# Seven-for-eight products of w_out for all batches of chunks 2 to 5, in an mLSTM cell with a cosine-gated feed-forward block

## The chip, the cores and the metric

The kernel runs on one core of one Trainium2 chip. The time is the device time of one execution in microseconds. Of the kernel before there are three runs, with a median of 536.95 us (536.02 to 537.94), and one profiled execution.

## The reference

Two blocks follow each other. The first is an mLSTM cell over 768 steps for 4 batches and 8 heads of 40 values: a state that decays by a forget gate and takes up an outer product at each step, is read with q, normalized and multiplied by an output gate. The second is a feed-forward block on its 3072 rows of 320 values. This change touches only the last product, that with w_out:

```python
x = np.ascontiguousarray(attn_out.transpose(0, 2, 1, 3)).reshape(B * S, H * D)   # (3072, 320)
h = x @ w_in                        # w_in (320, 2048)
g = h * np.cos(h)
return (g @ w_out).astype(np.float32)   # w_out (2048, 320)
```

All of it is in float32.

## The kernel before

**Tiling.** The 768 steps are cut into NC = 6 chunks of 128 steps; a cell is one chunk of one batch (all 8 heads), so there are 24 cells. The feed-forward block works on a chunk of all four batches at once, 4 x 128 = 512 rows. Its 2048 hidden values are 16 blocks of 128, taken two at a time: f2 = 0 to 7, each a pair.

**One slot.** For a pair, class Up multiplies x^T with the two blocks of w_in (L624 and L627) into two PSUM banks, the only two of the pool ps_u. ACT rounds (L632), DVE takes the fraction (L635), ACT takes the sine (L640), and DVE multiplies (L644, method gate) into the gated block g, 128 hidden values x 512 rows. gate reads the two banks last, so the next Up can have them only after that. I call the time of one Up and the work beside it a slot, T = 8c + f2 for chunk c.

**Order.** The order is written out by hand: both_parts(c, b) records an even slot (f2 = 2b) and an odd one (2b + 1), and each engine works through its own instructions in that order. Beside chunk c run the cells of chunk c + 1, a cell for each pair of slots. In an even slot TensorE does Up, the scores of the cell (L450), a step of w_out, then the values (L487, L493, into the two banks of pool ps_a which the scores also use); DVE does L635, weighs the scores (L456), subtracts for the next cell's decay (L372), multiplies the gates, and later normalizes (L507 to L519). In an odd slot TensorE does Up, the state's products (L589) and a step of w_out; DVE does L635, the state (L605), the gates, and transposes for the next cell (L411). Chunk 5 has no cells beside it, so its slots hold only Up and a step.

**x^T over DRAM.** The last 8 values of each head go from the normalized cell to DRAM (L523) and back (L526) into the third part of xT, which L627 reads.

**The product with w_out.** A step is `down(c, f2)`: it adds the pair's contribution for all four batches. In chunk 0 it is eight products of 320 columns (L757). From chunk 1 on, down_parted does batches 2 and 3 in that way (whole, four products of 320 columns), and batches 0 and 1 by Strassen's scheme in Winograd's form: the 2 x 2 blocks are two batches by the two blocks of the pair, and the two blocks by two halves of w_out's columns. Seven products P1 to P7 of 160 columns take the place of eight. They need four sums of blocks of g (`sums`, POOL, L683, in tiles "sg" of which there are two) and four differences of blocks of w_out for each pair (POOL, L662, made once in chunk 1). The products add up over all eight pairs in PSUM: P1, P2 and P6 in one bank of pool ps_o, P5, P3 and P4 in another, P7 beside batch 2's sum in a third; four banks in all. After the eighth pair ACT copies P1 (L726), seven additions on DVE (L731) make the two batches' rows, and ACT copies the whole ones (L708); SP stores them (L745).

down(c, f2) stands one slot after the pair's gates: pair f2's step is done in slot 8c + f2 + 1. So after the last Up two steps are done: pair 6, in the last slot, and pair 7 alone.

Of the kernel before, what the change touches and what calls it, by code (L numbers as in the profile page):

```python
# [11 lines left out]
FP = mybir.dt.float32  # L12
# [4 lines left out]
OP = mybir.AluOpType  # L17
# [6 lines left out]
TWO_PI = 2.0 * math.pi  # L24
# [5 lines left out]
def kernel(  # L30
# [20 lines left out]
    nc = tc.nc  # L51

    B, H, S, D = q.shape
    C = 128
    NC = S // C
# [3 lines left out]
    DM = H * D  # L59
    DFF = moe_w_in.shape[1]  # L60
    NF = DFF // 128
# [11 lines left out]
    const = ctx.enter_context(tc.tile_pool(name="const", bufs=1))  # L73
    wp = ctx.enter_context(tc.tile_pool(name="wp", bufs=1))
    p2 = ctx.enter_context(tc.tile_pool(name="p2", bufs=2))
    p3 = ctx.enter_context(tc.tile_pool(name="p3", bufs=3))
    p4 = ctx.enter_context(tc.tile_pool(name="p4", bufs=4))
    pb = ctx.enter_context(tc.tile_pool(name="pb", bufs=5))
# [3 lines left out]
    ps_u = ctx.enter_context(tc.tile_pool(name="ps_u", bufs=2, space=bass.MemoryType.PSUM))  # L82
    ps_o = ctx.enter_context(tc.tile_pool(name="ps_o", bufs=4, space=bass.MemoryType.PSUM))
# [48 lines left out]
    def parts(dst, bits):  # L132
        n = dst.shape[1]
        hi, lo = bits[:, 0:n, 1], bits[:, 0:n, 0].bitcast(U32)
        t = p2.tile([128, WQ], I32, name="wt", tag="wt")[:, 0:n]
        m = p2.tile([128, WQ], I32, name="wm", tag="wm")[:, 0:n]

        nc.scalar.activation(out=t.bitcast(FP), in_=hi.bitcast(FP), func=AF.Abs)

        nc.scalar.activation(out=m, in_=lo, func=AF.Copy, scale=2.0 ** -29)  # L140
        return dst, hi, t, m
# [139 lines left out]
        nc.scalar.copy(out=tab[:, 1, 2], in_=pg[:, 2 * R])  # L281
        nc.scalar.copy(out=tab[:, 1:R, 3], in_=pd)

    gp = ctx.enter_context(tc.tile_pool(name="gp", bufs=6))


    N = NC * B
# [320 lines left out]
    gs, po = {}, {}  # L608

    class Up:  # L610
# [23 lines left out]
        def rest(self, e):  # L634
            nc.vector.scalar_tensor_tensor(out=self.n[e].bitcast(FP), in0=self.pu[e], scalar=0.25, in1=self.n[e],  # L635
                                           op0=OP.add, op1=OP.subtract)
# [3 lines left out]
            nc.scalar.activation(out=r, in_=r, func=AF.Sin, scale=TWO_PI_DOWN)  # L640

        def gate(self, e):
            g = gp.tile([128, B * C], FP, name="g", tag="g")
            nc.vector.scalar_tensor_tensor(out=g, in0=self.pu[e], scalar=TWO_PI, in1=self.n[e].bitcast(FP),  # L644
                                           op0=OP.mult, op1=OP.mult)
            gs[self.c, 2 * self.f2 + e] = g

    DH = DM // 2
    Ts, sg = {}, {}

    def parted(c):
        return c > 0

    def differences(p, T):

        B11, B12, B21, B22 = (w_out_sb[:, 2 * p + e, ts(h, DH)] for e in range(2) for h in range(2))  # L660
        for i, (x, y) in enumerate(((B12, B11), (B22, T[:, 0]), (B22, B12), (T[:, 1], B21))):
            nc.gpsimd.tensor_tensor(out=T[:, i], in0=x, in1=y, op=OP.subtract)  # L662
        Ts[p] = T

    def two_differences(p):

        if p < 6:
            T = pc.tile([128, 2, 4, DH], FP, name="T", tag="bits")
            for e in range(2):
                differences(p + e, T[:, e])  # L670
        else:
            for e in range(2):
                differences(p + e, pb.tile([128, 4, DH], FP, name="T", tag="bits"))

    def sums(c, f2):

        if not parted(c):
            return
        S = p2.tile([128, 4, C], FP, name="sg", tag="wt")
        A11, A21, A12, A22 = (gs[c, 2 * f2 + e][:, ts(b, C)] for e in range(2) for b in range(2))  # L680
        for i, (x, y, op) in enumerate(((A21, A22, OP.add), (S[:, 0], A11, OP.subtract),
                                        (A11, A21, OP.subtract), (A12, S[:, 1], OP.subtract))):
            nc.gpsimd.tensor_tensor(out=S[:, i], in0=x, in1=y, op=op)  # L683
        sg[c, f2] = S

    def down_parted(c, f2):
        end = f2 == NF // 2 - 1
        if f2 == 0:

            po[c] = [ps_o.tile([128, 3 * DH + 32], FP, name="po", tag="o") for _ in range(4)]  # L690
        P1, P2, P6, P5, P3, P4 = (po[c][i // 3][:, ts(i % 3, DH)] for i in range(6))
        P7 = po[c][2][:, DM:DM + DH]
        g0, g1 = (gs[c, 2 * f2 + e] for e in range(2))
        w0, w1 = (w_out_sb[:, 2 * f2 + e] for e in range(2))
        S, T = sg[c, f2], Ts[f2]
        lo, hi = slice(0, DH), slice(DH, DM)

        def product(out, g, w, first=False):

            nc.tensor.matmul(out, g, w, start=(f2 == 0 and first), stop=end, skip_group_check=True)  # L700

        def whole(b):
            for e, (g, w) in enumerate(((g0, w0), (g1, w1))):
                product(po[c][b][:, 0:DM], g[:, ts(b, C)], w, e == 0)

        def whole_out(b):
            o = p2.tile([128, DM], FP, name="o_sb", tag="o_sb")
            nc.scalar.copy(out=o, in_=po[c][b][:, 0:DM])  # L708
            result(c, b, o)

        very_end = end and c == NC - 1
        if not very_end:
            for b in range(2, B):
                whole(b)
        product(P1, g0[:, 0:C], w0[:, lo], True)
        product(P2, g1[:, 0:C], w1[:, lo])
        product(P6, S[:, 1], T[:, 1])
        product(P7, S[:, 2], T[:, 2])
        product(P5, S[:, 0], T[:, 0], True)
        product(P3, S[:, 3], w1[:, hi])  # L720
        product(P4, g1[:, C:2 * C], T[:, 3])
        if not end:
            return None
        o2 = p2.tile([128, 2, DM], FP, name="o2", tag="wm")
        U = p1.tile([128, 2, DH], FP, name="hs", tag="hs")
        nc.scalar.copy(out=U[:, 0], in_=P1)  # L726
        for dst, x, y, op in ((o2[:, 0, lo], U[:, 0], P2, OP.add), (U[:, 0], U[:, 0], P6, OP.add),
                              (U[:, 1], U[:, 0], P7, OP.add), (U[:, 0], U[:, 0], P5, OP.add),
                              (o2[:, 0, hi], U[:, 0], P3, OP.add), (o2[:, 1, lo], U[:, 1], P4, OP.subtract),
                              (o2[:, 1, hi], U[:, 1], P5, OP.add)):  # L730
            nc.vector.tensor_tensor(out=dst, in0=x, in1=y, op=op)  # L731
        if very_end:
            for b in (3, 2):
                whole(b)

        def rest():
            for b in range(2):
                result(c, b, o2[:, b])
            for b in (3, 2):
                whole_out(b)  # L740

        return rest

    def result(c, b, o):
        nc.sync.dma_start(out=out[b * S + c * C:b * S + (c + 1) * C], in_=o)  # L745

    def down(c, f2):
        if parted(c):
            return down_parted(c, f2)
        if f2 == 0:  # L750
            po[c] = [ps_o.tile([128, DM], FP, name="po", tag="o") for _ in range(B)]

        order = [(f, b) for f in (2 * f2, 2 * f2 + 1) for b in range(B)]
        if f2 == NF // 2 - 1:
            order.sort(key=lambda fb: fb[1])
        for f, b in order:
            nc.tensor.matmul(po[c][b], gs[c, f][:, ts(b, C)], w_out_sb[:, f], start=(f == 0), stop=(f == NF - 1))  # L757
            if f == NF - 1:
                o = p2.tile([128, DM], FP, name="o_sb", tag="o_sb")
                nc.scalar.copy(out=o, in_=po[c][b])  # L760
                result(c, b, o)

    spot = const.tile([1, 1], FP, name="spot")
    nc.gpsimd.memset(spot, 0.0)
# [146 lines left out]
    def both_parts(c, b):  # L911
# [6 lines left out]
        begin = c == b == 0  # L918
        more = cell and n + 1 < N
        f2 = 2 * b  # L920
        up = Up(c, f2, cell_after_first if begin else None)
        if cell:
            scores(n)
# [14 lines left out]
        for e in range(2):  # L938
            up.sin(e)
            up.gate(e)  # L940
        sums(c, f2)
        if n == TURNED:
            turn_gates(n)
        if c == 0 and b == 1:
# [7 lines left out]
            out_join(*out_parts())  # L952
        if pieces:
            h = parts(*pieces.pop(0))
        rest = None
        if b == 0 and c > 0 and parted(c - 1):
            rest = down(c - 1, NF // 2 - 1)
        if begin or more and c > 0:
            decay(n + 1)
        elif more:  # L960
            decay_by_bias(n + 1)
        if f2 > 0:
            down(c, f2 - 1)
        elif rest:
            rest()
        elif c > 0:
            down(c - 1, NF // 2 - 1)
        if cell:
            if n + 2 < N:
                load(n + 2)  # L970
# [21 lines left out]
        sin_next()  # L992
        if pieces:
            h = parts(*pieces.pop(0))
        up = Up(c, f2 + 1)
        if cell:
            seam(n)
# [10 lines left out]
        for e in range(2):  # L1008
            up.sin(e)
            up.gate(e)  # L1010
        sums(c, f2 + 1)
        if more:
            weigh_k(n + 1)
        if c == 1 and b < B - 1:
            two_differences(2 * b + 2)
        if pieces:
            join(*parts(*pieces.pop(0)))
        down(c, f2)
        if pieces:
            join(*parts(*pieces.pop(0)))  # L1020
        if c == 0:
# [8 lines left out]
        if c == 0:  # L1030
            out_join(*h)
            if b == B - 1:
                two_differences(0)
                sigmoid(2)
                sin_next()
# [4 lines left out]
    with tc.manual_schedule():  # L1040
        first_cells()
        for c in range(NC):
            for b in range(B):
                both_parts(c, b)
        down(NC - 1, NF // 2 - 1)()


# [28 lines left out]
```

## Time and profile before

| | us |
|---|---|
| median of three runs | 536.95 |
| profiled execution | 536.09 |
| its span | 534.4 |
| Up (L624, L627), busy | 175.1 + 54.2 |
| w_out, chunk 0 (L757), busy | 36.6 |
| w_out, chunks 1 to 5 (L700), busy: 320 columns; 160 columns | 96.7; 39.4 + 28.3 + 17.4 + 17.4 |
| sums of g on POOL (L683), busy | 36.6 + 18.3 + 18.3 |
| gates on DVE (L644), busy; mean of one | 61.7; 0.684 |

The span is the profiled part of the execution; 1.7 us (536.09 - 534.4) lie outside it. Busy times of TensorE overlap each other, [...]so their sum is no measure of the span; starts of successive rows are the better measure. Each product of the program stands as two rows on TensorE: eight products of L757 are x16.

In pairs of slots, the starts of Up in the chain of waits are 20.62 us apart in chunks 1 to 3 and 20.19 in chunk 4; in chunk 5 each slot takes 8.74 us. DVE is busy 15.1 to 16.8 us of a pair, POOL 9.7 in chunk 1 and 5.7 in chunks 2 and 3.

### The profile page before, as it was taken

Reading aid. Unit: us, or ns where it says so; the run is one execution under the profiler, and the core shown is the slowest. Engines: PE = TensorE matmul, PEld = TensorE weight load, DVE = VectorE, ACT = ScalarE, POOL = GpSimd, SP = SyncE. Lnnn points to the kernel's source line nnn. Section 1 sums busy time; section 2 is a strip of 40 time slices with the busy share of each in tenths; the row PEclk is TensorE's granted clock in tenths of the full one; section 3 lists DMA queues with packets and bytes.
Section 4 is the critical chain, followed back from the end, with each engine's and each line's share of the span. In section 5 each row is a group of like instructions: output and inputs, shape, how many; then the busy total and the mean of one; then the engine's idle time right before and its main releaser. Section 6 shows DMA issues by size and latency. Waiting matters only on the chain.

```text
span 534.4 us, 10042 instructions
## 1 busy us (share of the span) xinstructions
PE 525.4 (98%) x3669; PEld 331.5 (62%) x3669; DVE 370.5 (69%) x734; ACT 262.2 (49%) x416; POOL 168.5 (32%) x305
## 2 busy tenths in 40 slices
PE   9999999999999999999999999999999999999997
PEld 6865566555575665666666666656656756656555
DVE  5888778889777677777767777767776765432323
ACT  3789696676632544543435534427335322332312
POOL 5532433434563353223222322422312211212121
PEclk9999999999999999999999999999999999999999
DMA  9999997952265725266536166536074000010001
GB/s 137 229 230 240 220 230 206 198 110 65 72 132 128 155 78 110 66 122 139 110 96 138 38 155 140 123 78 141 7 184 108 7 16 10 12 43 2 0 1 49
DMA packets 134857, 57.76 MB, mean 108 GB/s; under 512 B 70248, under 2 KB 130872, under 8 KB 134808
## 3 DMA queue, kind: packets, MB, share of 16 engines
q1 hardware_dynamic: 134664, 56.93, 47.9%
q8 instruction: 29, 0.48, 0.4%
q0 software_dynamic: 96, 0.18, 0.2%
q14 instruction: 20, 0.16, 0.1%
q10 hardware_dynamic: 48, 0.02, 0.0%
HBM read 50.76 MB, written 6.34 MB: 107 GB/s over the span
## 4 chain that ended last, share of the span: by engine, by line
PE 83%; DVE 6%; SPq 5%; ACT 2%; DMA 1%; issue 1%; POOL 1%; DVEq 0%; ACTq 0%; POOLq 0%
PE po L700 32%; PE pup L624 28%; PE pup L627 9%; PE po L757 4%; PE hp L493 3%; PE ps L450 3%; SPq L329 2%; PE hp L487 2%; DVE wt L148 1%; DVE wt L146 1%; PE pu L589 1%; DVE n L635 1%; DVE g L644 1%; DMA bits<-in_moe_w_in_dram 1%; DMA qs<-in_k_dram 1%
## 5 line engine op out<-in xcount | busy, mean ns | idle before, releaser
L624 PE MATMUL pup<-xT,w_in_sb 128*128 128x512 f32 x384 | 175.1, 598 | 1.8 <-DVE g L644 1.6
L632 ACT ACTIVATE n<-pup 128x512 int32<-128x512 f32 x96 | 52.0, 593 | 206.4 <-PE pup L627 206.4
L635 DVE SCALAR_TENSOR_TENSOR n<-pup,n 128x512 f32<-128x512 f32 x96 | 61.8, 685 | 118.2 <-ACT n L632 118.2
L700 PE MATMUL po<-w_out_sb,g 128*128 128x320 f32 (+1 forms) x480 | 118.6, 396 | 0.0
L624 PEld LDWEIGHTS pup<-xT,w_in_sb 128*128 128x128 f32 x384 | 69.7, 190 | 74.7 <-issue 64.3
L700 PEld LDWEIGHTS po<-w_out_sb,g 128*128 128x128 f32 x480 | 83.5, 190 | 36.7 <-issue 9.1
L683 POOL TENSOR_TENSOR sg<-g 128x128 f32<-128x128 f32 x80 | 36.6, 458 | 192.1 <-DVE g L644 190.7
L640 ACT ACTIVATE n<-n 128x512 f32<-128x512 f32 x96 | 58.9, 630 | 13.2 <-DVE n L635 13.2
L644 DVE SCALAR_TENSOR_TENSOR g<-pup,n 128x512 f32<-128x512 f32 x96 | 61.7, 684 | 2.5 <-ACT n L640 1.2
L627 PE MATMUL pup<-xT,w_in_l 64*128 64x512 f32 x192 | 54.2, 641 | 0.6 <-DVE w_in_l L149 0.6
L373 POOL TENSOR_SCALAR_AFFINE_SELECT E<-E 128x1024 f32<-128x1024 f32 x19 | 20.8, 1092 | 96.4 <-DVE E L372 67.9
L700 PE MATMUL po<-T,sg 128*128 128x160 f32 x240 | 39.4, 300 | 0.0
L627 PEld LDWEIGHTS pup<-xT,w_in_l 64*128 64x128 f32 x192 | 14.4, 184 | 37.0 <-issue 34.1
L757 PE MATMUL po<-w_out_sb,g 128*128 128x320 f32 x128 | 36.6, 439 | 0.5 <-POOL w_out_sb L149 0.4
L700 PEld LDWEIGHTS po<-T,sg 128*128 128x128 f32 x240 | 34.8, 190 | 0.2
L411 DVE STREAM_TRANSPOSE t<-qs 128x512 f32<-128x512 f32 x34 | 34.8, 1099 | 0.0
L381 ACT ACTIVATE E<-E 128x1024 f32<-128x1024 f32 x21 | 22.2, 1058 | 20.8 <-POOL E L373 19.0
L456 DVE TENSOR_TENSOR E<-ps,E 128x512 f32<-128x512 f32 x48 | 30.7, 680 | 2.5 <-ACT E L381 2.1
L450 PEld LDWEIGHTS ps<-t,t 40*128 40x128 f32 (+1 forms) x384 | 25.1, 188 | 9.7 <-issue 9.2
L757 PEld LDWEIGHTS po<-w_out_sb,g 128*128 128x128 f32 x128 | 23.7, 190 | 10.3 <-POOL w_out_sb L149 1.1
L900 ACT ACT_TABLE_LOAD x20 | 25.7, 1283 | 0.4
L450 PE MATMUL ps<-t,t 40*128 40x128 f32 (+1 forms) x384 | 25.8, 274 | 0.0
(154 smaller groups left out, 641.0 us busy)
## 6 DMA issues: line engine op xcount, KB each, us to landing
E<-M_d SPq DMA_DIRECT2D x22, 512.0 KB
bits<-in_moe_w_in_dram SPq DMA_DIRECT2D x40, 128.0 KB
bits<-in_moe_w_out_dram SPq DMA_DIRECT2D x8, 640.0 KB
room<-G_d SPq DMA_DIRECT2D x34, 128.0 KB
ks<-in_k_dram SPq DMA_DIRECT2D x24, 160.0 KB
vs<-in_v_dram SPq DMA_DIRECT2D x24, 160.0 KB
o<-in_o_gate_dram SPq DMA_DIRECT2D x68, 40.0 KB
qs<-in_q_dram SPq DMA_DIRECT2D x34, 80.0 KB
```

The costliest lines, as they stand in the source:

```text
L411: nc.vector.transpose(out=dst.rearrange("r p (t x) -> r p x t", x=T4), in_=src.rearrange("r p (x d) -> r p x d", x=T4)[:, :, :, 0:32])
L450: nc.tensor.matmul(ps[j][:, p], kT[r, p], qT[r, p], start=True, stop=True)
L456: nc.vector.tensor_tensor(out=w, in0=pss[n][j], in1=w, op=OP.mult)
L624: nc.tensor.matmul(pu, w_in_sb[:, i, ts(block(f2, e), 128)], x(i), start=(i == 0), stop=False)
L627: nc.tensor.matmul(pu, w_in_l[r, f2], x(NK, r), start=False, stop=True)
L632: nc.scalar.activation(out=self.n[e], in_=self.pu[e], func=AF.Copy, bias=0.25)
L635: nc.vector.scalar_tensor_tensor(out=self.n[e].bitcast(FP), in0=self.pu[e], scalar=0.25, in1=self.n[e], op0=OP.add, op1=OP.subtract)
L640: nc.scalar.activation(out=r, in_=r, func=AF.Sin, scale=TWO_PI_DOWN)
L644: nc.vector.scalar_tensor_tensor(out=g, in0=self.pu[e], scalar=TWO_PI, in1=self.n[e].bitcast(FP), op0=OP.mult, op1=OP.mult)
L683: nc.gpsimd.tensor_tensor(out=S[:, i], in0=x, in1=y, op=op)
L700: nc.tensor.matmul(out, g, w, start=(f2 == 0 and first), stop=end, skip_group_check=True)
L757: nc.tensor.matmul(po[c][b], gs[c, f][:, ts(b, C)], w_out_sb[:, f], start=(f == 0), stop=(f == NF - 1))
```

## The change

From chunk 2 on, batches 2 and 3 are also done in seven products, with sums of their own. The seven products of two batches (s = 0 for batches 0 and 1, s = 1 for 2 and 3) now take three banks and are not held at the same time as the other two batches': s = 0 of chunk c is done in the second half of the chunk's time and s = 1 in the first half of the next one's. A half-step is (c, s, p, in parts or whole), and a table says in which slot T each is done:

```diff
+    for p in range(NP):
+        put(9 + p, (1, 0, p, IN_PARTS))
+        put((9, 11, 13, 15, 17, 17, 18, 18)[p], (1, 1, p, WHOLE))
+        put((19, 20, 20, 21, 22, 22, 23, 24)[p], (2, 0, p, IN_PARTS))
+        for c in range(2, NC):
+            if c > 2:
+                put(8 * c + 5 + p // 2, (c, 0, p, IN_PARTS))
+            put(8 * c + 9 + p // 2, (c, 1, p, WHOLE if c == NC - 1 and p == NP - 1 else IN_PARTS))
+    LAST = max(plan)
```

Chunk 1 keeps its batches 2 and 3 whole, and so does the very last half-step. By this table slots 10, 12, 14, 16, 19, 21, 23 and 24 hold one half-step, and all others from slot 9 on two. The last slot with an Up is 47; slots 48 to 52 come after it.

The gated blocks are kept longer, so they lie in 12 units of 128 x 512 (six of their own as before, six in room that the loading of weights leaves): one unit holds a pair's two blocks for two batches. From chunk 1 on, gate therefore writes two halves of 256 columns to two units instead of 512 columns to one:

```diff
-            g = gp.tile([128, B * C], FP, name="g", tag="g")
-            nc.vector.scalar_tensor_tensor(out=g, in0=self.pu[e], scalar=TWO_PI, in1=self.n[e].bitcast(FP),
-                                           op0=OP.mult, op1=OP.mult)
-            gs[self.c, 2 * self.f2 + e] = g
...
+            for s in range(2):
+                if e == 0:
+                    gs[c, f2, s] = spare.pop(0)
+                nc.vector.scalar_tensor_tensor(out=gs[c, f2, s][:, ts(e, W)], in0=self.pu[e][:, ts(s, W)], scalar=TWO_PI,
+                                               in1=n[:, ts(s, W)], op0=OP.mult, op1=OP.mult)
```

The sums are made at the start of the slot that uses them, ahead of its Up in the order; on POOL, but on DVE in slots 50 to 52:

```diff
-        S = p2.tile([128, 4, C], FP, name="sg", tag="wt")
-        A11, A21, A12, A22 = (gs[c, 2 * f2 + e][:, ts(b, C)] for e in range(2) for b in range(2))
...
+        for c, s, p, in_parts in plan.get(T, ()):
+            if in_parts:
+                S = p2.tile([128, 4, C], FP, name="sg", tag="wt")
+                A11, A21, A12, A22 = (gs[c, p, s][:, ts(i, C)] for i in range(4))
+                engine = nc.vector if T > 8 * NC + 1 else nc.gpsimd
...
     def both_parts(c, b):
...
+        slot = NF // 2 * c + f2
+        sums(slot)
         up = Up(c, f2, cell_after_first if begin else None)
...
-        sums(c, f2)
...
+        rests = []
+        ends = any(step[2] == NP - 1 for step in plan.get(slot, ()))
+        if ends:
+            rests = down(slot)
...
+        sums(slot + 1)
         up = Up(c, f2 + 1)
```

New functions: in_parts does the seven products, whole the four, sums_room takes the three banks (four in chunk 1), and put_together holds ACT's copy and DVE's seven additions, which are as before; it now runs once for each s in parts, nine times instead of five. In the very last slot it also adds the last whole half-step's two sums, which lie in ps_u's banks:

```diff
+    def down(T):
...
+        steps = sorted(plan[T], key=lambda step: (step[3], step[:3]))
...
+        for c, s, p, parted in steps:
+            end = p == NP - 1
+            if parted:
+                in_parts(c, s, p)
+                if end:
+                    o2 = put_together(c, s)
+                    rests.append(lambda c=c, s=s, o2=o2: [result(c, 2 * s + b, o2[:, b]) for b in range(2)])
...
+    def very_last():
+
+        (c, s, p, parted), (_, _, z, _) = plan[LAST]
+        in_parts(c, s, p)
+        sums = [ps_u.tile([128, DM], FP, name="pl", tag="up") for _ in range(2)]
+        for b in range(2):
+            whole(c, s, z, b, sums[b], True)
+        put_together(c, s, sums)
...
-        down(NC - 1, NF // 2 - 1)()
+        for T in range(NC * NP, LAST):
+            sums(T)
+            for rest in down(T):
+                rest()
+        sums(LAST)
+        very_last()
```

Chunk 0, the cells and all loads are as before.

## The prediction

> **What bounds the kernel now.** I read the page first (busy shares, then the chain that ended last), then the waits of TensorE, then the chain in order of time, and last the timelines of one slot of each kind. Slots are those of the description above: slot T = 8c + f2 is one Up with the work beside it; even slots also hold a cell's scores and values.
>
> ```profile
> PE 525.4 (98%) x3669; PEld 331.5 (62%) x3669; DVE 370.5 (69%) x734; ACT 262.2 (49%) x416; POOL 168.5 (32%) x305
> ...
> PE 83%; DVE 6%; SPq 5%; ACT 2%; DMA 1%; issue 1%; POOL 1%; DVEq 0%; ACTq 0%; POOLq 0%
> ...
> PE pup L624 <- DVE g L644: 1.6, 3, 0.7
> ...
> 128.03 3.43 PE pup L624 x8
> ...
> 133.41 4.50 PE po L757 x16
> ...
> 139.53 3.63 PE pup L624 x8
> ...
> 144.65 4.25 PE po L700 x22
> 148.90 3.43 PE pup L624 x8
> ...
> 160.15 3.63 PE pup L624 x8
> ```
>
> PE is busy 98% and in all the span waits 1.6 us for gates (third line, all in chunk 0). From 128 us on the chain (start, us, what) is nothing but PE. So products taken off PE are time gained, as long as PE does not come to wait. The last lines give the gain: a step on four whole batches is 4.50 us, one with two batches in seven products 4.25. The starts of Up agree: slot 8, whole, is 139.53 - 128.03 = 11.50 us, slot 10, half in parts, 160.15 - 148.90 = 11.25. Two batches of a step thus cost w = 2.25 us whole and p = 2.00 in parts: 0.25 saved.
>
> What PE would wait for is hidden today. A slot even (10, from Up's start at 148.74) and odd (11, from 160.08), by the timeline (start, us, engine, line, what):
>
> ```profile
> 154.06 1.29 DVE L635 SCALAR_TENSOR_TENSOR n<-pup,n 128x512 f32<-128x512 f32 x2 [2.26 <-ACT n L632]
> ...
> 155.26 1.27 DVE L456 TENSOR_TENSOR E<-ps,E 128x512 f32<-128x512 f32 x2
> ...
> 156.46 1.21 DVE L372 TENSOR_TENSOR E<-E,tab 128x1024 f32<-128x1024 f32 x1
> ...
> 157.59 1.28 DVE L644 SCALAR_TENSOR_TENSOR g<-pup,n 128x512 f32<-128x512 f32 x2
> ...
> 158.47 0.67 PE L487 MATMUL hp<-room,st 40*32 40x128 f32 x32
> ...
> 160.08 3.70 PE L624 MATMUL pup<-xT,w_in_sb 128*128 128x512 f32 x8
> ...
> 165.21 2.96 PE L700 MATMUL po<-w_out_sb,g 128*128 128x320 f32 x12
> 165.56 1.29 DVE L635 SCALAR_TENSOR_TENSOR n<-pup,n 128x512 f32<-128x512 f32 x2 [1.76 <-ACT n L632]
> ...
> 166.77 0.67 DVE L605 TENSOR_TENSOR st<-st,pu 40x164 f32<-40x164 f32 x2
> 167.46 1.29 DVE L644 SCALAR_TENSOR_TENSOR g<-pup,n 128x512 f32<-128x512 f32 x2
> ...
> 169.37 1.88 PE L624 MATMUL pup<-xT,w_in_sb 128*128 128x512 f32 x4
> ```
>
> The pool ps_u has two banks, so the next Up cannot start before the gates have read both. DVE runs without a gap from L635 to the gates. In the odd slot the gates end 8.67 us after Up's start (168.75) and the next Up comes at 9.29: only 0.6 us to spare, and it is the w_out step at 165.21 that fills the time.
>
> [...]each product here stands twice in the trace, and 16 rows of 320 columns in 4.50 us are 281 ns each and 14 of 160 in 2.00 are 143: [...]proportional to columns, so seven half-width products for four full ones save a little under 1/8. [...](512 columns 685 ns, 256 columns 395), so gates cut in two cost more. [...]here the copy of P1 at 527.46 comes after P6, third product in that bank, not after P1. [...]
>
> **The change part by part.**
> *Products.* Chunks 2 to 5 give 31 half-steps in parts instead of whole (the 32nd stays whole): 31 x 0.25 = -7.75 us. The last step before waits about 0.25 for its sums on POOL (14 narrow rows take 526.33 to 528.48, 2.15, where 515.68 to 517.58 is 1.90); that goes: -0.25. Together -8.0.
>
> *Work moved.* One half-step instead of two stands in slots 10, 12, 14, 16 and 24 (even) and 19, 21, 23 (odd); the 2.25 us left out of each comes back at the end, where five steps follow the last Up instead of one. In the sum of PE's work it is neutral; what counts is whether PE can use the time. It cannot fully:
> - Gates in halves: the nearest row is L516 (256 columns, one operand in PSUM), two in 0.71 us. Four then take 0.71 for the first 512 columns and 1.34 in all, if they overlap as L516's do (0.395 each, 0.315 apart); 1.58 if not. I take 1.34. After a gate PE starts 0.15 later (chunk 0: first gate 105.53 to 106.21, Up 106.37).
> - Odd slot, one half-step: PE is free at 5.13 + 2.00 = 7.13 after Up's start. Gates start at 7.38, so the first bank is free at 8.09 and Up starts at 8.24; the second bank, wanted 0.43 later, is there at 8.87, another 0.2, partly absorbed: 8.40 in effect. So 0.89 is gained of 2.25; 1.36 lost, x3 = 4.1.
> - Even slot, one half-step: w_out ends at 5.48 + 2.00 = 7.48. L487 needs ps_a's two banks, which L456 leaves at 7.79: it starts at 7.86, and with 1.61 for L487 and L493 PE is free at 9.47. Gates start at 8.85: banks at 9.71 and 10.34, Up at 9.87 in effect against 11.34. So 1.47 gained, 0.78 lost, x5 = 3.9.
> - Full slots: two half-steps in parts take 4.00, PE is free at 9.13 (odd) while the first bank is ready at 8.24: nothing lost. In chunk 5 (8.74 us a slot) the gates are ready 7.7 after Up's start, PE at 8.5: nothing.
>
> *Putting together twice a chunk.* ACT's copy and DVE's seven additions (2.34 us, 527.78 to 530.12) now come nine times, not five, in even slots after the gates, before L507's run of 3.8 us. In full slots DVE then ends at 16.3 where the next L635 is due at 16.6: hidden. After slot 24, which is short, L635 of slot 25 is 1.1 us late and PE gets its banks at 9.56 against 9.13: 0.4 lost. In slot 17 the two whole half-steps (4.5) cover it. The result stores wait at the head of SP's queue before load(n+2); in chunk 2's first pair they do so today without a wait on PE.
>
> *POOL's sums*, four more per slot (1.83 us): POOL is busy 5.7 of 20.6 us in a pair of chunk 2, 9.8 in chunk 1. A sum's buffer is free 0.3 us before the half-step two before it ends; Up (4.5 us) covers even slots, E's select and then Up the odd ones. Cost nothing; if the cover is gone, PE waits up to 1.8 in a slot.
>
> *xT over DRAM.* At chunk 3's first Up the last rows of xT are issued at 292.77 and L627 reads them at 296.64. Short slot 23 wants them 0.9 earlier; their landing isn't shown: 0 to 0.9, I take 0.3.
>
> *The end.* Slots 48 to 52 have no Up between. P7 of slot 49 needs a bank that the additions of slot 48 still read: they end about 3.94 after the last half-step's start (as 526.33 to 530.12 before, plus 0.15), PE is there at 2.00 + 0.86: 1.1 lost. Sums keep pace (1.83 on POOL, about 1.2 on DVE, against 2.00). At the very end an addition of 320 columns takes the place of ACT's copy (0.46 after PE's end): about 0.73, so 0.3.
>
> Sum: -8.0 + 4.1 + 3.9 + 0.4 + 0.3 + 1.1 + 0.3 = +2.1 us. The profiled execution has 536.09 (span 534.4), which becomes 538.2; the median of the three runs is 0.86 above it, so I give 539.0.
>
> **Rivals.**
> 1. *The short slots hide the gate chain after all (faster).* The mechanism is the one wait on ps_u's banks in the eight short slots, priced at 8.0 in my sum. If PE loses nothing there, the result is -5.9 (531); at a third of my price, -3.3, about 534. It decides from a mean loss under 0.74 us a slot, where mine is 1.00. For it: starts of PE rows are modelled, and the gates' halves let the first bank go early. Against it: 58 to 106 us already show Up waiting for gates at their end, and DVE has no gap in the chain.
> 2. *The cover of POOL and DVE is thinner (much slower).* Gates in halves at 1.58 and sums or additions late: if the slots with additions (seven) and POOL's full slots each lose 0.5, some 5 us more: 544. For it: DVE would have only 0.3 us of room in slots with additions. Against it: POOL's idle time.
> 3. *Nothing gained, nothing lost:* the saving is 0.35 a half-step (8 rows at 281 ns against 1.90), 31 x 0.1 = 3.1 more, so -1.0: 536. Against it: the slots' starts, 0.25 both ways.
>
> **How the numbers follow.** Forecast 0.50, rival 1 0.25, rival 2 0.15, rival 3 0.10. About 0.3% (1.6 us) is what this kernel's measurement can tell. The forecast's own range is 536.5 to 541.5 (DMA 0 to 0.9, gates 1.34 to 1.58 in eight slots up to 1.6, additions 1); within it about a quarter lies within 0.3%. Faster: 0.2 of rival 1 and 0.05 of the rest; within: 0.14 + 0.05 + 0.06; slower: the other half. Range 532.5 to 544.5.
>
> **What would show it.** PE waiting for the gates' line in slots 19, 21, 23 about 1.1 us each and in the five even ones 0.2 (with 0.4 before L487 on L456); Up to Up 8.4 and 9.9 us there; full pairs of 20.1 us instead of 20.63; chunk 5's slots 8.5 instead of 8.74; one wait near 1.1 in the stretch after the last Up. Wrong if PE's waits after 128 us are in sum under 5 us, or if full slots show any.

## The result, and the profile after

| us | before | after |
|---|---|---|
| median (range) of the four executions each | 537.26 (536.02 to 537.94) | 555.23 (549.51 to 557.11) |
| profiled execution | 536.09 | 549.51 |
| its span | 534.4 | 547.8 |

The ratio is 1.032, 95% interval 1.024 to 1.040. I had predicted 539.0, with 532.5 to 544.5 as the range. The executions of the changed kernel lie further apart than those of before, and the profiled one is the quickest of its four, so its trace has 13.4 of the median's 18 us to show.

The page of the changed kernel: busy times, granted clock in 40 slices of 13.7 us, and the chain of waits by engine.

```profile
PE 526.2 (96%) x3855; PEld 349.6 (64%) x3855; DVE 396.6 (72%) x864; ACT 260.5 (48%) x412; POOL 209.3 (38%) x409
...
PEclk9899999999999999999999999996999999999999
...
PE 72%; DVE 11%; DMA 7%; ACT 3%; issue 2%; POOL 1%; SPq 1%; DVEq 0%; POOLq 0%; ACTq 0%
```

TensorE was 98% busy and 83% of the chain. Now it is 96% and 72%, and DMA stands in the chain with 7%. Two slices of the clock are low, the second and the 28th. Which waits of TensorE are new is told by its list of waits (total, times, longest):

```profile
PE pup L628 <- issue: 6.0, 1, 6.0
PE pup L625 <- DVE g L653: 2.7, 3, 0.9
PE pup L628 <- DMA xT<-X_d: 1.8, 2, 1.5
PE pup L625 <- DVE g L648: 1.6, 3, 0.7
...
PE pup L625 <- DVE gg L653: 0.8, 1, 0.8
```

L625 and L628 are L624 and L627 of before, L653 the gates from chunk 1 on, and L648 those of chunk 0, whose 1.6 us stood before too. The three waits of 0.9 for L653 stand behind the short odd slots, and the one of 0.8 ahead of slot 32. The two lines of L628 are the part of Up that reads what has gone through DRAM. Only one of the two names its releaser; "issue" says that the profile shows none for the 6.0 us.

From the starts of Up in the timeline of TensorE each slot's length follows. For slots 19, 20 and 21 of the changed kernel (start, us, what):

```profile
238.67 3.70 PE L625 MATMUL pup<-xT,w_in_sb 128*128 128x512 f32 x8
...
246.86 3.70 PE L625 MATMUL pup<-xT,w_in_sb 128*128 128x512 f32 x8 [0.90 <-DVE g L653]
...
258.06 2.41 PE L625 MATMUL pup<-xT,w_in_sb 128*128 128x512 f32 x5
```

Slot 19, odd and short, is 246.86 - 238.67 = 8.19; slot 20, even and full, 11.20. All slots together, read in this way:

| slots | before | predicted | after |
|---|---|---|---|
| even, one half-step (10, 12, 14) | 11.34 | 9.87 | 9.65, 9.70, 9.71 |
| odd, one half-step (19, 21, 23) | 9.28 | 8.40 | 8.19, 8.15, 8.19 |
| a full pair (26 + 27) | 20.62 | 20.1 | 20.20 |
| chunk 5, each | 8.74 | 8.5 | 8.49 |
| 16 | 11.34 | 9.87 | 10.24 |
| 24 | 11.34 | 9.87 | 11.34 |
| 31 | 9.28 | 9.03 | 9.95 |
| 32 | 11.34 | 11.1 | **21.17** |

So nearly everything is where the prediction had it or better, and four slots are not. Slot 32 alone is 10.1 us too long.

**Slot 32.** The timeline of TensorE there, of the changed kernel:

```profile
367.89 3.70 PE L625 MATMUL pup<-xT,w_in_sb 128*128 128x512 f32 x8 [0.76 <-DVE gg L653]
377.59 2.76 PE L628 MATMUL pup<-xT,w_in_l 64*128 64x512 f32 x4 [6.00 <-issue]
379.43 2.62 PE L451 MATMUL ps<-t,t 40*128 40x128 f32 x16
```

TensorE stands still for 6.0 us ahead of L628, and then L628's four rows take 2.76 where they take 1.13 elsewhere, and the scores (L451) 2.62 where they take 1.06. The windows say why (stretch, its length, busy time and count of PE, PEld, DVE, ACT, POOL, then granted clock, DMA share, GB/s):

```profile
377.60:381.00 3.40, 3.40 (x17) 2.81 (x17) 0.64 (x1) 1.16 (x2) 0.00 (x0) 0.50 0.02 7
381.00:385.00 4.00, 4.00 (x18) 3.77 (x17) 3.99 (x8) 1.29 (x3) 0.76 (x1) 0.50 0.00 0
385.00:389.00 4.00, 4.00 (x83) 3.50 (x81) 2.32 (x9) 2.50 (x3) 3.66 (x9) 1.00 0.01 4
```

For 7.4 us behind the wait the clock is half. The slot loses 6.0 by waiting and nearly all of the other 4.1 by running slowly: 7.4 us at half the clock are 3.7 us lost.

**Why xT is late.** The queue of SyncE (SP), which issues the loads and stores in the order in which they were recorded, from slot 28 on. First before, where Up of slot 28 starts at 334.36:

```profile
336.63 0.39 SPq L323 DMA_DIRECT2D qs<-in_q_dram  x1
...
344.79 10.49 SPq L305 DMA_DIRECT2D o<-in_o_gate_dram  x16
355.38 1.21 SPq L523 DMA_DIRECT2D X_d<-room  x2
...
369.22 1.20 SPq L523 DMA_DIRECT2D X_d<-room  x2
372.72 1.26 SPq L526 DMA_DIRECT2D xT<-X_d  x2
```

Then after, where Up of slot 28 starts at 326.73:

```profile
326.62 1.26 SPq L527 DMA_DIRECT2D xT<-X_d  x2
338.86 0.84 SPq L742 DMA_DIRECT2D out_dram<-o  x2
339.75 0.45 SPq L324 DMA_DIRECT2D qs<-in_q_dram  x1
...
346.85 9.88 SPq L306 DMA_DIRECT2D o<-in_o_gate_dram  x16
356.82 1.21 SPq L524 DMA_DIRECT2D X_d<-room  x2
...
369.87 1.21 SPq L524 DMA_DIRECT2D X_d<-room  x2
375.39 1.26 SPq L527 DMA_DIRECT2D xT<-X_d  x2
```

Before, SP's loads for the next cell begin 2.3 us after Up's start. After, SP issues nothing from 327.9 to 338.86, because the two stores of `result` (L742) stand ahead of load(n + 2) and wait for the last addition of put_together; the loads begin 13.0 us after Up's start. This is also the one slot of chunk 3 where load_o's 16 loads of o_gate stand behind the others, and they hold SP for another 9.9 us. X_d of this cell therefore goes out 30 us after its slot's Up instead of 21. The loads of slot 30 find SP still at that work, and the last read of X_d back into xT is issued 28.5 us after its slot's Up (slot 30, 346.85) instead of 17.7. In the kernel before it was issued 372.72 and L627 ran at 379.14. In the changed one L628 starts 2.2 us after the issue; by that measure before had 379.14 - 372.72 - 2.2 = 4.2 us of slack at slot 32, and the change took 10.8.

SP also waits for the store of X_d before it issues the read of it: its list of waits has L527 <- DMA X_d<-room with 53.0 us in 20 waits, the longest 4.3. L527 follows L524 by 5.5 us in the last two lines (3.5 before), and whatever is recorded behind it waits too.

### The profile page after: what moved, and what is told of

Same layout as the page of the kernel before. It is cut to its first block, busy times and chain, and to the rows that moved or that the text cites. A ratio compares the mean times of both kernels' runs of the same rounds, so it can differ in the third digit from the quotient of the medians.

```text
span 547.8 us, 10620 instructions
## 1 busy us (share of the span) xinstructions
PE 526.2 (96%) x3855; PEld 349.6 (64%) x3855; DVE 396.6 (72%) x864; ACT 260.5 (48%) x412; POOL 209.3 (38%) x409
## 4 chain that ended last, share of the span: by engine, by line
PE 72%; DVE 11%; DMA 7%; ACT 3%; issue 2%; POOL 1%; SPq 1%; DVEq 0%; POOLq 0%; ACTq 0%
PE po L721 25%; PE pup L625 24%; PE pup L628 8%; PE po L817 4%; DMA X_d<-room 3%; PE ps L451 3%; PE hp L494 2%; DVE n L636 2%; PE hp L488 1%; PE ph L476 1%; ACT n L633 1%; DMA qs<-in_q_dram 1%; DMA bits<-in_moe_w_in_dram 1%; DVE wt L148 1%; DVE E L373 1%
## 5 line engine op out<-in xcount | busy, mean ns | idle before, releaser
L625 PE MATMUL pup<-xT,w_in_sb 128*128 128x512 f32 x384 | 175.6, 599 | 5.6 <-DVE g L653 2.7
L625 PEld LDWEIGHTS pup<-xT,w_in_sb 128*128 128x128 f32 x384 | 69.5, 190 | 79.9 <-issue 63.3
L721 PE MATMUL po<-T,sg 128*128 128x160 f32 x426 | 70.3, 301 | 0.0
L628 PE MATMUL pup<-xT,w_in_l 64*128 64x512 f32 x192 | 57.0, 651 | 8.4 <-issue 6.0
L721 PEld LDWEIGHTS po<-T,sg 128*128 128x128 f32 x426 | 62.5, 192 | 0.0
L717 POOL TENSOR_TENSOR sg<-g 128x128 f32<-128x128 f32 x66 | 30.1, 457 | 66.5 <-PE po L721 44.3
L717 POOL TENSOR_TENSOR sg<-gg 128x128 f32<-128x128 f32 x66 | 30.1, 457 | 43.0 <-PE po L721 39.6
L628 PEld LDWEIGHTS pup<-xT,w_in_l 64*128 64x128 f32 x192 | 15.7, 187 | 45.8 <-issue 42.3
L721 PE MATMUL po<-w_out_sb,g 128*128 128x160 f32 (+1 forms) x180 | 38.1, 340 | 0.0
L721 PE MATMUL po<-w_out_sb,gg 128*128 128x160 f32 (+1 forms) x168 | 34.8, 334 | 0.0
L721 PEld LDWEIGHTS po<-w_out_sb,g 128*128 128x128 f32 x180 | 27.9, 189 | 10.8 <-issue 6.8
L451 PEld LDWEIGHTS ps<-t,t 40*128 40x128 f32 (+1 forms) x384 | 28.2, 197 | 9.2 <-issue 8.5
L457 DVE TENSOR_TENSOR E<-ps,E 128x512 f32<-128x512 f32 x48 | 30.7, 679 | 2.5 <-ACT E L382 2.1
L653 DVE SCALAR_TENSOR_TENSOR g<-pup,n 128x256 f32<-128x256 f32 x82 | 30.6, 414 | 1.1 <-issue 0.6
L721 PE MATMUL po<-w_out_sb,sg 128*128 128x160 f32 x142 | 31.0, 300 | 0.0
```

What stands on the lines that cost most here:

```text
L451: nc.tensor.matmul(ps[j][:, p], kT[r, p], qT[r, p], start=True, stop=True)
L457: nc.vector.tensor_tensor(out=w, in0=pss[n][j], in1=w, op=OP.mult)
L625: nc.tensor.matmul(pu, w_in_sb[:, i, ts(block(f2, e), 128)], x(i), start=(i == 0), stop=False)
L628: nc.tensor.matmul(pu, w_in_l[r, f2], x(NK, r), start=False, stop=True)
L653: nc.vector.scalar_tensor_tensor(out=gs[c, f2, s][:, ts(e, W)], in0=self.pu[e][:, ts(s, W)], scalar=TWO_PI, in1=n[:, ts(s, W)], op0=OP.mul ...
L717: engine.tensor_tensor(out=S[:, i], in0=x, in1=y, op=op)
```

## The experiments

Theory A: SP's order alone makes the losses. The stores wait for DVE and hold up the loads behind them; nothing is wrong with the shorter slots as such. Theory B: the shorter slots bring the loads closer together than the transfers can follow. Each time below is a median, with the ratio to the kernel before on the same chip.

**The changed kernel again** (no edit).

> The changed kernel once more, for a second profile beside the times. Both theories: about 549 to 557. Theory A (SP's order: the stores of slot 28 wait for the additions on DVE with the loads and the o_gate loads queued behind them, xT is late at slot 32, TensorE idles 6 us and then runs at a lower granted clock) expects the same long gap between the Ups of slots 32 and 33 (over 17 us), and in a slower execution either a longer one or a second gap at slot 16 or 24. Theory B (the transfers as a whole can't follow the faster slots) expects gaps at changing places.

555.23 us, 1.031 (1.026 to 1.036). The trace this time is of an execution of 560.6 us, 11 above the first one. Its slot 32 is 21.35, and slot 24, 11.34 in the first trace, is 16.90: TensorE waits 2.86 us for xT there. About half of the 11 us is that; the other half is in chunk 0, which the change leaves as it was: slot 8 starts 6.0 us later than in the first trace (135.40 instead of 129.42). I take from it only that a second chunk's start has the same wait at times, as the trace of "o_gate earlier" below has too.

**Stores last.** Only the place of the stores in SP's order moves, from ahead of load(n + 2) to the end of the even slot's work:

```diff
         elif slot and not ends:
             down(slot)
-        for rest in rests:
-            rest()
         if cell:
...
                 turn_blocks(n + 1)
+        for rest in rests:
+            rest()
         h = ()
```

> All stores of results in even slots are put behind the cell's loads and its X_d stores on SP; nothing else moves. Theory A: slot 32 takes 11.1 us instead of 21.2, slot 24 some 9.8 instead of 11.3, slot 16 about 9.8 instead of 10.2; 536 to 538. Theory B: no change, 549 or more, since the amount and pace of the transfers are the same.

538.18 us, 1.0014 (0.9993 to 1.0036). 17 of the 18 us are gone. SP and TensorE from slot 28 (Up at 329.72) to slot 32, in this kernel's timelines:

```profile
330.54 0.34 SPq L324 DMA_DIRECT2D qs<-in_q_dram  x1
...
337.57 9.30 SPq L306 DMA_DIRECT2D o<-in_o_gate_dram  x16
346.97 1.21 SPq L524 DMA_DIRECT2D X_d<-room  x2
...
351.63 0.92 SPq L742 DMA_DIRECT2D out_dram<-o  x2
...
367.49 1.26 SPq L527 DMA_DIRECT2D xT<-X_d  x2
```

```profile
369.96 3.60 PE L625 MATMUL pup<-xT,w_in_sb 128*128 128x512 f32 x8
373.49 1.13 PE L628 MATMUL pup<-xT,w_in_l 64*128 64x512 f32 x4
```

The loads begin 0.8 us after Up again, the read of X_d is out 2.5 us before Up of slot 32 starts, and L628 follows without a wait. Slot 32 takes 11.09 and slot 24 takes 9.82. Against what was expected (about 9.8 in slot 16), one gap is left in the execution of this trace (541.5 us): slot 16 takes 14.80. There L628 waits 1.77 us for xT, and the windows show the clock at 0.73 from 212.6 to 216 and 0.50 from 216 to 220. No store stands in SP's queue between slots 9 and 16 in either kernel, so this one is not the stores' doing; load_o's loads of chunk 3 stand there too, in slot 12. The executions range from 535.2 to 545.5, those of the kernel before from 535.9 to 540.4, so the gap is hardly in all of them; only this one was traced.

**o_gate earlier.** The other half of the same collision: the stores stay where they are, and load_o(5) is issued in slot 26 instead of 28.

```diff
-            if b == B - 2 and c + 2 < NC:
+            if b == (B - 3 if c == 3 else B - 2) and c + 2 < NC:
                 load_o(c + 2)
```

> The 16 loads of o_gate for chunk 5's cells stand one pair of slots earlier (slot 26 instead of 28); the stores stay ahead of the loads. Theory A: the 10 us that SP needs for them no longer add to the 10 us it waits for the additions, so slot 32's gap goes (11 to 13 us instead of 21), the ones at 16 and 24 stay: 538 to 543. Theory B: no change.

543.42 us, 1.011 (1.009 to 1.014), 0.4 above the range expected. Slot 32 takes 11.09 in its trace, so the wait needs both: late stores and 16 loads behind them. Chunk 3's start, slot 24, is as it was in this kernel, and takes 15.77 in this execution:

```profile
294.12 1.11 PE L628 MATMUL pup<-xT,w_in_l 64*128 64x512 f32 x3 [2.79 <-DMA xT<-X_d]
...
295.16 2.32 PE L451 MATMUL ps<-t,t 40*128 40x128 f32 x15
```

**The same wait in the kernel before.** In slot 28, nothing else: DVE copies 128 values of the cell's result, SP stores them in a scratch tensor, and load(n + 2) stands behind that store. It adds this copy and store to the kernel before.

```diff
-            if n + 2 < N:
+            late = (c, b) == (3, 2)
+            if n + 2 < N and not late:
                 load(n + 2)
...
+            if late:
+                nc.vector.tensor_copy(out=probe, in_=hps[n][1][:, 1, 0:1])
+                nc.sync.dma_start(out=probe_d, in_=probe)
+                load(n + 2)
```

> The kernel before, with one thing added in slot 28 alone: a store of 128 values which DVE copies after the values' products, and the loads of cell n + 2 behind it. Theory A: SP's loads start about 10 us later there, of which some 4 us are slack before slot 32, so TensorE waits about 5 us for xT and then runs some us at a lower clock: 7 to 10 us slower than before, 544 to 547. Theory B: no change, 537, for the slots are no faster than before.

553.38 us, 1.031 (1.027 to 1.034). TensorE's and SP's lists of waits, the first two lines and the last two:

```profile
PE pup L627 <- DMA xT<-X_d: 6.6, 1, 6.6
PE pu L589 <- DVE room L516: 4.1, 1, 4.1
```

```profile
SPq L983 <- DVE room L507: 9.8, 1, 9.8
...
SPq L325 <- DMA probe_d<-probe: 5.4, 1, 5.4
```

A single store in this place, with the two waits of SP that come with it, is enough to bring the old kernel, with its old slots, to the time of the changed one. It cost more than I expected, for two reasons. SP waited a second time, 5.4 us, in the middle of the loads for the small store to land. And slot 31 became 15.16 instead of 9.28 by another path, on which the state's products (L589) waited 4.1 us for DVE's normalizing (L516). I take DVE to have been held there by the late store of X_d; the lists above don't show it, but in the changed kernel L508 waits 2.28 us for that store, up to 359.45. Slot 32 became 22.06, 10.7 more than before; that part is the stall of the changed kernel (10.1). Theory B isn't needed for the large loss.

**o_gate spread.** Stores last, and load_o in three parts over three pairs:

```diff
-            if b == B - 2 and c + 2 < NC:
-                load_o(c + 2)
+            if c + 2 < NC:
+                if c > 0 and b < B - 1:
+                    load_o(c + 2, ((0,), (1, 2), (3,))[b])
+                elif b == B - 2:
+                    load_o(c + 2)
```

> The changed kernel with the result stores issued at the end of the even slot's work (as in e1_late_stores), and load_o's 16 loads of one chunk spread over three of its pairs (4, 8, 4) instead of all 16 in the third, from chunk 1 on. Theory A (SP's order alone makes the losses): the last gap, the 1.8 us wait at slot 16 and the half clock behind it, goes too; slot 16 takes 9.7 instead of 14.8, slots 24 and 32 stay at 9.8 and 11.1: 538.2 - 5.1 = 533, range 532 to 535. Theory B (there are too many bytes for the shortened slots): the waits only move to another slot, and the time stays at 537 or above.

536.75 us, 0.9998 (0.997 to 1.003). The slots came out as Theory A has them: 16, 24 and 32 take 9.72, 9.81 and 11.09, and no wait for xT is left in TensorE's list. The time lies between the two theories' ranges, 3.7 us above my number for A, because I had taken the 5.1 us of slot 16 off the median of "stores last", though they were seen in one of its higher executions. In its trace the last Up starts 373.84 us after that of slot 8 and the end follows 31.6 after that: 405.5, against 389.72 + 16.8 = 406.5 before. That is the change without its stall: 1.0 us gained in this trace, and nothing that the comparison of times could tell from zero.

**The short slots.** Three more on top of that, to test the model of the gates: chunk 2's products in slots 19, 19, 20, 21, 21, 22, 23, 24, which makes two odd short slots even; the gates ahead of other work on DVE in the short slots; and both.

```diff
-        put((19, 20, 20, 21, 22, 22, 23, 24)[p], (2, 0, p, IN_PARTS))
+        put((19, 19, 20, 21, 21, 22, 23, 24)[p], (2, 0, p, IN_PARTS))
```

```diff
-        if begin or more and c > 0:
+        short = 9 < slot < 25 and len(plan[slot]) == 1
+        if (begin or more and c > 0) and not short:
             decay_exponents(n + 1)
         for e in range(2):
             up.sin(e)
             up.gate(e)
+        if (begin or more and c > 0) and short:
+            decay_exponents(n + 1)
...
-        if cell:
+        if cell and not short:
             state(n)
...
+        if cell and short:
+            state(n)
```

> e5_o_gate_spread with the products of the first two batches of chunk 2 in slots 19, 19, 20, 21, 21, 22, 23, 24: slots 19 and 21 hold two half-steps and 20 and 22 one. By the prediction's model an odd short slot stands 1.15 above its products' saving and an even one 0.6 (from the changed kernel's slots), so two swaps give 2 x 0.57 = 1.1 us against e5_o_gate_spread. If the short slots are bound by something other than the chain of the gates, the swap gives nothing.

> e5_o_gate_spread with, in the short slots alone, VectorE's gates ahead of decay_exponents (even slots) or of state (odd slots). The prediction's account of a short slot: the Up behind it waits for the gates, and these wait for VectorE. If so the five even ones (10, 12, 14, 16, 24) go from 9.7 towards 9.15, and the three odd ones (19, 21, 23) from 8.2 to 7.8: 5 x 0.5 + 3 x 0.4 = 3.7 us less than e5_o_gate_spread, near 529.5. If the sines of ScalarE end the wait instead, under 1 us.

> e6_even_short and e7_gates_first together: seven even short slots at 9.15 and one odd at 7.8: 1.1 + 7 x 0.5 + 0.4 = 5.0 us less than e5_o_gate_spread, near 528, and faster than the kernel before by 1.7%.

| | time, us | ratio (interval) | first Up of slot 8 to last Up, us |
|---|---|---|---|
| o_gate spread | 536.75 | 0.9998 (0.997 to 1.003) | 373.84 |
| + even short slots | 535.25 | 0.996 (0.994 to 0.998) | 372.90 |
| + gates first | 535.23 | 0.995 (0.993 to 0.998) | 372.46 |
| + both | 535.67 | 0.998 (0.995 to 1.000) | 372.00 |

The differences in time among these four are inside their intervals, so I read the last column. The swap was expected to give 1.1. The swapped slots give 1.24 (pair 19 + 20 goes from 8.20 + 11.19 to 9.03 + 9.72, pair 21 + 22 likewise); the column has 0.94, because slot 16 took 10.06 instead of 9.72 in this trace. The gates first give 1.38, not 3.7, and both together 1.84, not 5.0. The odd slots go to 7.68 to 7.75, as expected, the even ones only to 9.46 to 9.63. In slot 10 of that kernel, by its timeline:

```profile
155.10 1.28 DVE L457 TENSOR_TENSOR E<-ps,E 128x512 f32<-128x512 f32 x2
...
156.30 1.41 DVE L653 SCALAR_TENSOR_TENSOR gg<-pup,n 128x256 f32<-128x256 f32 x4
157.62 1.21 DVE L373 TENSOR_TENSOR E<-E,tab 128x1024 f32<-128x1024 f32 x1
158.04 1.12 PE L625 MATMUL pup<-xT,w_in_sb 128*128 128x512 f32 x2
```

The gates are ahead of L373 now, and the next Up starts with no wait in brackets: another bound than the gates holds the slot. The prediction names one that fits: the values' products (L488) need the banks that the weighing (L457) reads, so TensorE is free 9.47 us after Up's start. Here L457 ends 7.80 after Up's start (156.38 - 148.58), and the next Up comes at 9.46. My expectation of 9.15 had left that out. Behind slots 16 and 24 the work that was put off comes late, and slots 17 and 25 grow from 9.69 and 9.64 to 9.89 and 10.26.

**Without the gates first in slots 16 and 24.** One line (`short = 9 < slot < 24 and b > 0 and ...`); and, in a second kernel, two products of zeros (`warm(2)`) ahead of values(0) in the start as well.

> e8_both without the gates first in slots 16 and 24, whose next slots (17 and 25) e8_both's trace shows 0.25 and 0.6 us longer: Up-start to Up-start over slots 8 to 46 371.6 instead of 372.0 in e8_both, 389.7 in the kernel before; with the 14.8 us more of products after the last Up (31.6 against 16.8) that is 3.3 us less than before, a ratio of 0.994. If chunk 5's longer end or chunk 0's start took the gain, 1.000.

> e9_gates_first_less with two matrix products of zeros ahead of values(0) in the start, where TensorE waits 0.27 to 1.22 us for VectorE in the ten profiles so far, and where the granted clock fell to 0.54 to 0.61 for 4 us in the two with the longest waits (1.09 and 1.22). Theory C (a wait of about 1 us is enough for a lower clock): no lower clock there, chunk 0 ends at most as late as in the other profiles, and the time is 0 to 1 us below e9_gates_first_less with fewer high runs. If the lower clock has another cause, it is seen as before.

534.32 us, 0.996 (0.994 to 0.998), and 534.77 us, 0.996 (0.994 to 0.998). Slot 25 is back at 9.63. Slot 16 of the first took 10.51, with a wait of 0.65 us at L628, so this start of a chunk is still tight. From slot 8 to the last Up its trace has 372.24 us, not the 371.6 expected (the second kernel's has 371.52). The first beats the kernel before by 2.2 us in the medians (536.56 there), less than the 3.3 expected; by its own trace it is 2.6. The second shows no lower clock in the start, but most others don't either; it can't decide what it was meant for, and is no faster.

## Why the prediction was wrong

**The step that failed** is the sentence on the stores: "The result stores wait at the head of SP's queue before load(n+2); in chunk 2's first pair they do so today without a wait on PE." It named the queue and cost it at nothing, by one place where it is harmless today. It is not the wait alone: in the kernel before, too, SP idles 11 to 14 us ahead of its stores in slots 16, 24 and 32, but no loads of o_gate stand behind those. The change adds places, and in one of them, slot 28, the queue behind the stores holds more: the 16 loads of o_gate, X_d, and, through these, the next chunk's first Up. What I should have listed is everything behind the waiting store and its deadline: stores 12.1 us after Up's start (338.86 - 326.73), then 7.1 us of loads, 9.9 us of o_gate, X_d. In sum the last read of X_d came 10.8 us later against a slack of 4.2, and TensorE stood still for 6.0; the prediction had 0. "Stores last" and the wait put into the kernel before show it from both sides.

**xT over DRAM** was the step where this had to appear. It looked at chunk 3's first Up alone, by the 0.9 us that the slot before is shorter, and took 0.3. The traces of the changed kernel show waits for xT of 0.3, 1.5 and 6.0 us in one execution and 2.9 at chunk 3 in another, and behind the two long ones slow rows (L451 takes 2.62 and 2.38 us instead of 1.06; the clock behind the first is 0.50), which no step had.

**The rest of the sum held.** With the stall taken away (o_gate spread):

| term, us | predicted | measured | from |
|---|---|---|---|
| odd short slots | 4.1 | 3.5 | 3 x (8.19 - 7.03) |
| even short slots | 3.9 | 3.2 | 9.66, 9.72, 9.72, 9.72, 9.81, each less 9.09 |
| slot 25 | 0.4 | 0.6 | 9.64 - 9.03 |
| xT at chunk 3 | 0.3 | 0 | no wait for xT in its list |
| wait in slot 49 | 1.1 | 0 | below |
| the very end | 0.3 | 0.1 | 3.7 instead of 3.6 from the last product to the end |

(7.03 and 9.09 are the old slots, 9.28 and 11.34, less the 2.25 moved out.) With -8.0 for the products, the sum becomes -0.6, and the trace has -1.0 by starts of Up. The short slots ended 0.15 to 0.2 us earlier than the model of the gates said, although four gates took 1.41 and not 1.34. One sign that I had named for a wrong model did come: TensorE's waits after 128 us are under 5 us in sum (the list of "o_gate spread" has 3.2). In the even slots the loss shows less as waits than as longer rows: in slot 10 L488 takes 0.94 instead of 0.67.

**The wait in slot 49.** The changed kernel's timeline of TensorE at the end has half-steps 1.90 apart throughout (526.57, 528.47, 530.37), while the additions of slot 48 run until 530.25. So P7 did not wait for them. The bank that the pool gave it was not looked up, so why is open.

**The rivals.** The rival on the short slots decided from a mean loss under 0.74 us a slot; it is 0.84 (6.7 over eight). (Its -3.3 at a third of my price is -3.2 by its own numbers.) DVE's and POOL's covers held. The rival with the large loss had its place in DVE and POOL; that of the runs is in SP's queue, and none of mine was.

**The sum of the first trace.** Against "o_gate spread", slots 16, 24, 31 and 32 have 0.5, 1.5, 0.9 and 10.1 too much, 13.0 together. Chunk 0 ends 1.6 later than before, which is the next section's matter. 534.4 - 1.0 + 13.0 + 1.6 = 548.0; the span is 547.8. Where the other 5.7 us of the median lie is open. Slot 24 is 5.6 us longer in the second trace and 4.4 in that of "o_gate earlier", but chunk 0 ends 6.0 us later in the second trace as well.

## What to carry to other kernels

When work moves, write down for each queue of the issuing engine what stands behind every instruction that now waits, until the first consumer with a deadline, and measure the slack of that one: two stores that take 0.8 us and wait for an addition held 29 loads here. Put stores of results last in a stage's order; in these traces TensorE never waits for them ahead of the end. And price a stall of TensorE at more than its length, since the clock behind it can cost as much again or more (about 4 us behind 6.0, 3.3 behind 1.77), though it need not (nothing behind 1.83).

## What the runs showed of the hardware

**Half the clock came behind waits of 1.1 us and more, but not behind all of them.** Slot 16 has both cases, first in "stores last" with a wait of 1.77 us, then in "o_gate earlier" with one of 1.83:

```profile
212.62 1.26 PE L628 MATMUL pup<-xT,w_in_l 64*128 64x512 f32 x3 [1.77 <-DMA xT<-X_d]
```

```profile
213.25 1.25 PE L628 MATMUL pup<-xT,w_in_l 64*128 64x512 f32 x3 [1.83 <-DMA xT<-X_d]
```

Behind the first wait came the clocks of 0.73 and 0.50, which cost 14.80 - 9.72 - 1.77 = 3.3 us besides the wait. Behind the second the rows kept their usual length (six rows of L721 take 0.98 us, behind the first 1.81), and the slot took 11.63, just the wait more than 9.72. The start of the kernel has a shorter case, the wait ahead of the first values. Before, and then after, by TensorE's timeline:

```profile
14.14 1.98 PE L475 MATMUL ph<-vs,E 128*128 128x41 f32 x16 [0.69 <-DVE E L456]
16.05 1.16 PE L450 MATMUL ps<-t,t 64*128 64x128 f32 x16
```

```profile
14.14 1.98 PE L476 MATMUL ph<-vs,E 128*128 128x41 f32 x16 [1.09 <-DVE E L457]
16.05 1.82 PE L451 MATMUL ps<-t,t 64*128 64x128 f32 x16
```

The same rows take 1.16 or 1.82; the clock from 16 to 20 us is 1.00 or 0.57. In the nine traces with windows of the clock there, the wait in this place is 0.27 to 0.81 us in seven, with a clock of 1.00 behind it, and 1.09 and 1.22 in two (the changed kernel and "stores last"), with 0.54 to 0.61 for 4 us. That is an order in the data; no run set this wait by itself. The lower clock also accounts for the 1.6 us that chunk 0 lost in the first trace, where the change does nothing. But length alone does not decide: besides slot 16 of "o_gate earlier", TensorE waited 1.49 us in slot 24 of the changed kernel, with the clock at 1.00 from 285 to 301, and 1.8 us for the gates in chunk 0 of "even short slots", whose mean clock over the span is 1.000. The windows of three kernels give the length of the stretches of half clock, if the clock is taken as either 0.50 or 1.00 within a window: 3.4 and 10.2 us in the changed kernel (16.4 to 19.8 and 374.8 to 385.0), 3.4 and 6.8 in "stores last" (16.2 to 19.6 and 214.1 to 220.9), and 10.2 behind the wait put into the kernel before (389.2 to 399.5). Half of such a stretch is what it costs, by this estimate, as far as TensorE has work in it: 3.4 at slot 16, where 3.3 was measured, and 1.7 at the start, where it was 1.6. What sets these lengths, and when such a stretch begins, no run here shows.
